# Two buffers for q and k, one PSUM buffer per product, and a reordered end in a sigmoid attention followed by a mixture of depths

## The chip, the cores and the metric

The kernel runs on one core of one Trainium2 chip. The metric is the device time of one execution in microseconds (us). Names of engines: PE is TensorE (PEld its weight loads), DVE is VectorE, ACT is ScalarE, POOL is GpSimd, SP is SyncE, which here only issues DMAs.

## The reference

```python
# q, k, v: (8, 12, 448, 64) float32;  capacity = 128;  D = 12*64 = 768;  F = 1024
scores = scale * np.matmul(q, k.transpose(0, 1, 3, 2)) - np.log(S)
attn = 1.0 / (1.0 + np.exp(-scores))
x = np.matmul(attn, v).transpose(0, 2, 1, 3).reshape(B, S, H * D)   # (8, 448, 768)

scores = np.einsum('bsd,d->bs', x, w_gate)
out = x.copy()
for b in range(B):
    top_idx = np.argpartition(-scores[b], capacity)[:capacity]      # 128 of 448 rows
    xe = x[b, top_idx]
    ye = np.maximum(xe @ w1, 0.0) @ w2                              # 768 -> 1024 -> 768
    g = 1.0 / (1.0 + np.exp(-scores[b, top_idx]))
    out[b, top_idx] = x[b, top_idx] + g[:, None] * ye
```

## The kernel before

**Attention.** The 96 heads are cut into 24 groups of four; a group is one index i of `load`, `turn` and `raws`. A stage s (0 to 11) works on groups 2s and 2s+1. `load(i)` fetches k and q of a group with two DMAs from SP, `turn(i)` transposes them on DVE into `kT` and `qT`, and a stage's seven `unit`s multiply q by k on PE into PSUM (line 269) and apply the sigmoid on ACT (line 277). `values` multiplies by v (line 304), one stage later for three of its four parts, into two PSUM tiles called `o`; `take` transposes the result on DVE into `x_b` (line 319), and that frees the `o` tiles.

**Choosing rows.** A batch b has three groups. When its x is whole, `gate` sums the scores, `spread` copies them over all partitions through DRAM (tile `rep`), `store` writes x to DRAM with four DMAs from SP, `ranking` counts on DVE how many scores are above each (lines 378 and 381), `place` sends the ranks through DRAM into `spot`, and `choose` finds the 128 rows and gathers them into `xe` with an indirect DMA from POOL. `copy_out` copies all of x to the output, and `scatter` overwrites the chosen rows at the end.

**The two products with w1 and w2.** Two batches (a pair p) are done together by a scheme of seven products of quarter matrices instead of eight: `first(p, key)` for w1, `second(p, key)` for w2, keys 1 to 7, each with sums before (rows in `rows_t`) and after (`first_sums`, `second_sums`, on DVE, ACT and POOL). The sums of weights are made once, kept in DRAM, and fetched by `lend` into attention tiles that are free for a while. `WORK` says at which stage and unit a product stands: (8, 5) is the gap behind unit 5 of stage 8, in which PE has nothing of the attention before the next unit. The last pairs follow in `rest`, after the attention.

**What sets the order.** The order of each engine is the order in the program; no scheduler moves anything, and semaphores make an engine wait where data or a buffer is missing. SP's DMAs stand in one line too: a DMA that waits holds up all behind it. DVE is likewise one line: `turn`, `ranking`, `take`, `gate_part` and the sums of products stand behind each other.

**Two places that the change touches.** In `raw` there is one buffer for k and one for q, so `load(i)` can start only when `turn(i-1)` has read the group before. And `bank` hands out the two halves of one PSUM tile to two products one after the other (`half`).

Of the kernel before, what the change touches and what calls it, by code (L numbers as in the profile page):

```python
# [9 lines left out]
F32 = mybir.dt.float32  # L10
# [7 lines left out]
def kernel(  # L18
# [40 lines left out]


    const = ctx.enter_context(tc.tile_pool(name="const", bufs=1))
    raw = ctx.enter_context(tc.tile_pool(name="raw", bufs=1))
    vals = ctx.enter_context(tc.tile_pool(name="vals", bufs=1))
    head = ctx.enter_context(tc.tile_pool(name="head", bufs=2))
    dram = ctx.enter_context(tc.tile_pool(name="dram", bufs=B, space=bass.MemoryType.DRAM))
# [24 lines left out]
    def load(i):  # L90

        if i >= NQ:
            return
        if i == 1:
            both = moe.tile([P, 7 * KH * P], F32, name="rows_t")
            raws[i] = [both[:, n * TB * Dh:(n + 1) * TB * Dh] for n in range(2)]
        else:
            raws[i] = [raw.tile([P, TB * Dh], F32, name=f"raw_{nm}") for nm in "kq"]
        for t, src in zip(raws[i], (k, q)):
            nc.sync.dma_start(  # L100
                out=t, in_=bass.AP(tensor=src.tensor, offset=src.offset + i * 4 * S * Dh,
                                   ap=[[TB * Dh, P], [1, TB * Dh]]))
# [40 lines left out]
    def load_weights(m):  # L143
        n = KH if m == 1 else FH
        w = (w1_sb, w2_sb)[m - 1]
        held = [(0, 0), (0, 1), (1, 1)] if m == 1 else [(0, 0), (1, 0), (1, 1)]
        left = (1, 0) if m == 1 else (0, 1)
        room = moe.tile([P, 7 * FH * P], F32, name="hidden")
        a, b = room[:, :QW], room[:, QW:2 * QW]
        c = moe.tile([P, 7 * KH * P], F32, name="rows_t")[:, :QW]  # L150
# [234 lines left out]
    def place(b):  # L385

        nc.vector.tensor_add(place_s[:, :NC], above, level)
        by_col = moe.tile([P, TT], F32, name="by_col")
        nc.vector.transpose(by_col, place_s)
        ranks = dram.tile([P, TT], F32, name="ranks")  # L390
        queue(b).dma_start(out=ranks, in_=by_col)
        spot = moe.tile([P, 4, NC * TT], F32, name="spot")
        queue(b).dma_start(
            out=spot, in_=bass.AP(tensor=ranks.tensor, offset=ranks.offset,
                                  ap=[[0, P], [TT * TT, 4], [1, NC * TT]]))
        st[b]["spot"] = spot.rearrange("p m c -> p (m c)")[:, :S]

    def choose(b):
# [19 lines left out]
            idx.append(at)  # L418
        gt = moe.tile([P, 1], F32, name="gate", bufs=4)
        nc.scalar.activation(gt[:n], picked[1][:n], AF.Sigmoid)  # L420
        xe = moe.tile([P, D], F32, name="xe", bufs=4)
        nc.gpsimd.indirect_dma_start(
            out=xe[:n], out_offset=None, in_=st[b]["x_d"][:, :],
            in_offset=bass.IndirectOffsetOnAxis(ap=row[:n, 0:1], axis=0))
        st[b].update(idx=idx, gate=gt, xe=xe)

    pairs, half = {}, [None]

    def bank(where):
        if half[0] is None:  # L430
            half[0] = banks(where)
            return half[0][:, 0]
        t, half[0] = half[0], None
        return t[:, 1]

    def turn_rows(b, where="o"):


        n = CAP
        p, odd = divmod(b, 2)  # L440
        if not odd:
            t = moe.tile([P, 7 * KH * P], F32, name="rows_t")
            pairs[p] = {"x": t.rearrange("p (m k n) -> p m k n", m=7, k=KH)}
# [12 lines left out]
        for dst, y, z in ((4, 2, 0), (2, 3, 2), (5, 3, 4), (6, 1, 5)):  # L456
            eng.tensor_tensor(out=x[:, dst, :, :n], in0=x[:, y, :, :n], in1=x[:, z, :, :n],
                              op=ALU.subtract)

    ROWS1 = {1: 0, 2: 1, 3: 3, 4: 6, 5: 4, 6: 5, 7: 2}

    def first(p, key, where="o"):
        n = CAP
# [85 lines left out]
    def scatter(b, m=None):  # L551
# [11 lines left out]

    WORK = {
# [10 lines left out]
    }  # L575

    LENT = {5: [(1, 7), (1, 6)], 6: [(1, 5), (1, 3), (2, 4)], 7: [(2, 5), (2, 6), (2, 7)],
            8: [(1, 7), (1, 6)], 9: [(1, 5), (1, 3)], 10: [(2, 4), (2, 5), (2, 6)],
            11: [(2, 7), (1, 7), (1, 6)]}

    def begin(item, where="o"):

# [5 lines left out]

    def do(item, where="o"):
        if item[0] == "t":  # L590
            half[0] = None
            turn_rows(item[1], where)
        elif item[0] == "s":
            for x in range(2):
# [40 lines left out]
    def gap(s, n):  # L635
        if n < 3 and s > 0:
            values(s - 1, n + 1)
            if n == 2:
                turns[0] = 1
                half[0] = None  # L640
# [59 lines left out]
    def stream():  # L700
        for b in range(B):
            routed(b)
        load(0)
        load(1)
        zero = moe.tile([P, NC * P], F32, name="spot")
        nc.vector.memset(zero, 0.0)
        nc.vector.memset(bias_s, NEG_LOG_S)
        turn(0)
        load(2)
        load_v(0)  # L710
        warm = banks(1)
        for _ in range(3):
# [51 lines left out]
```

## Time and profile before

| | |
|---|---|
| runs | 551.33, 552.72, 556.01 us; median 552.72 us |
| profiled execution | 556.21 us, of which the span of the trace is 554.2 us |
| mean granted PE clock of the span | 0.944 |
| busy: PE, PEld, DVE, ACT, POOL | 465.5, 273.7, 293.8, 184.6, 92.5 us |
| DMA | 104.19 MB, mean 188 GB/s |

A group of the profile names the line, the engine, the operation, out<-in tiles, the shape and the number of instructions. In a timeline a row is: start and length in us, engine, line, operation, tiles, and in brackets the idle time of that engine just ahead and what ended it. PE's full clock is 2.4 GHz, and 1.2 GHz is the lower of its two levels (granted clock 0.5).

### The profile page before, as it was taken

Reading aid. Unit: us, or ns where it says so; the run is one execution under the profiler, and the core shown is the slowest. Engines: PE = TensorE matmul, PEld = TensorE weight load, DVE = VectorE, ACT = ScalarE, POOL = GpSimd, SP = SyncE. Lnnn points to the kernel's source line nnn. Section 1 sums busy time; section 2 is a strip of 40 time slices with the busy share of each in tenths; the row PEclk is TensorE's granted clock in tenths of the full one; section 3 lists DMA queues with packets and bytes.
Section 4 is the critical chain, followed back from the end, with each engine's and each line's share of the span. In section 5 each row is a group of like instructions: output and inputs, shape, how many; then the busy total and the mean of one; then the engine's idle time right before and its main releaser. Section 6 shows DMA issues by size and latency. Waiting matters only on the chain. (4 is left out here: it accounts for less than half of the span.)

```text
span 554.2 us, 14369 instructions
## 1 busy us (share of the span) xinstructions
PE 465.5 (84%) x6326; PEld 273.7 (49%) x6326; DVE 293.8 (53%) x637; ACT 184.6 (33%) x240; POOL 92.5 (17%) x92
## 2 busy tenths in 40 slices
PE   8998839794998968985899997977998978586884
PEld 3554314362646534532446775543565467246842
DVE  3346593928529285428338385456445474542351
ACT  4754613452544531432253443341353201001000
POOL 7191560110000000400102000400001202411002
PEclk9999987896999988997999998998999997799998
DMA  8887996796277838674786837956567769816701
GB/s 258 282 270 266 334 246 180 132 263 144 49 243 189 168 82 245 109 240 148 170 294 180 146 118 190 165 215 195 134 209 189 144 175 237 308 34 234 278 14 43
DMA packets 134281, 104.19 MB, mean 188 GB/s; under 512 B 97996, under 2 KB 115644, under 8 KB 133964
## 3 DMA queue, kind: packets, MB, share of 16 engines
q1 hardware_dynamic: 130940, 89.07, 59.2%
q0 software_dynamic: 3280, 14.21, 8.4%
q8 instruction: 49, 0.80, 0.6%
q14 instruction: 12, 0.10, 0.1%
HBM read 82.67 MB, written 31.60 MB: 206 GB/s over the span
## 5 line engine op out<-in xcount | busy, mean ns | idle before, releaser
L269 PE MATMUL psc<-qT,kT 32*64 32x448 f32 x2496 | 161.0, 553 | 17.3 <-DVE qT L251 12.9
L304 PE MATMUL o<-attn_d,raw_v 32*64 32x448 f32 x1152 | 131.1, 541 | 0.6 <-ACT o L307 0.3
L304 PE MATMUL o<-attn_u,raw_v 32*64 32x448 f32 x1152 | 127.0, 540 | 1.4 <-ACT o L307 0.8
L277 ACT ACTIVATE attn_u<-psc,bias_s 128x896 f32<-128x896 f32 x86 | 81.9, 1004 | 121.4 <-PE psc L269 121.3
L269 PEld LDWEIGHTS psc<-qT,kT 32*64 32x64 f32 x2496 | 66.0, 134 | 82.8 <-issue 52.4
L277 ACT ACTIVATE attn_d<-psc,bias_s 128x896 f32<-128x896 f32 x70 | 66.7, 1004 | 57.8 <-PE psc L269 57.7
L304 PEld LDWEIGHTS o<-attn_u,raw_v 32*64 32x64 f32 x1152 | 51.3, 133 | 30.4 <-issue 21.0
L244 DVE STREAM_TRANSPOSE kT<-raw_k 128x384 f32<-128x384 f32 x46 | 23.8, 555 | 73.6 <-DMA raw_k<-in_k_dram 44.2
L304 PEld LDWEIGHTS o<-attn_d,raw_v 32*64 32x64 f32 x1152 | 50.2, 133 | 21.2 <-issue 18.9
L533 PE MATMUL o<-w_sb,hidden 128*128 128x384 f32 x72 | 34.9, 645 | 25.9 <-DVE x_b L319 15.6
L319 DVE STREAM_TRANSPOSE x_b<-o 128x448 f32<-128x448 f32 x48 | 26.8, 616 | 50.1 <-PE o L304 50.0
L544 DVE SCALAR_TENSOR_TENSOR xe<-o,gate,xe 128x384 f32<-128x384 f32 x43 | 24.5, 612 | 43.7 <-PE o L533 43.7
L474 PE MATMUL o<-rows_t,attn_d 128*128 128x128 f32 x264 | 36.0, 300 | 10.2 <-DVE hidden L484 5.7
L484 DVE TENSOR_TENSOR hidden<-o,hidden 128x512 f32<-128x512 f32 x25 | 16.7, 688 | 48.1 <-PE o L474 47.9
L474 PEld LDWEIGHTS o<-rows_t,attn_d 128*128 128x128 f32 x264 | 34.2, 213 | 15.0 <-DVE hidden L484 6.7
L533 PEld LDWEIGHTS o<-w_sb,hidden 128*128 128x128 f32 x72 | 17.3, 251 | 42.2 <-issue 34.1
L519 POOL TENSOR_TENSOR hidden<-hidden 128x512 f32<-128x512 f32 x12 | 16.5, 1393 | 129.8 <-ACT hidden L487 129.5
L327 DVE TENSOR_TENSOR scr<-x_b,wg_b 128x448 f32<-128x448 f32 x48 | 36.5, 761 | 1.0
L474 PE MATMUL o<-rows_t,w_sb 128*128 128x128 f32 x264 | 32.3, 279 | 3.4 <-ACT rows_t L451 1.9
L474 PEld LDWEIGHTS o<-rows_t,w_sb 128*128 128x128 f32 x264 | 30.3, 192 | 8.2 <-issue 3.1
L487 ACT ACTIVATE hidden<-hidden 128x512 f32<-128x512 f32 x15 | 9.5, 630 | 66.5 <-DVE hidden L484 66.5
L330 DVE TENSOR_REDUCE gate_p<-scr 128x14 f32<-128x448 f32 x48 | 29.8, 621 | 1.7
(102 smaller groups left out, 454.7 us busy)
## 6 DMA issues: line engine op xcount, KB each, us to landing
attn_d<-sum SPq DMA_DIRECT2D x52, 384.0 KB, 7.6
x_d<-x_b SPq DMA_DIRECT2D x32, 336.0 KB, 6.9
out_dram<-x_d SPq DMA_DIRECT2D x8, 1344.0 KB, 9.3
raw_k<-in_k_dram SPq DMA_DIRECT2D x23, 448.0 KB, 5.0
raw_q<-in_q_dram SPq DMA_DIRECT2D x23, 448.0 KB, 5.7
raw_v<-in_v_dram SPq DMA_DIRECT2D x48, 192.0 KB, 8.9
w_sb<-in_moe_w_dram SPq DMA_DIRECT2D x6, 768.0 KB, 12.4
sum<-hidden POOLq DMA_DIRECT2D x6, 768.0 KB, 6.4
```

What stands on the lines that cost most here:

```text
L244: nc.vector.transpose(kT[i][:, e, :HK], sk[:, e, :HK].rearrange("p (m c) d -> p c m d", c=NF))
L269: nc.tensor.matmul(psc[h // 2][y * Dh:(y + 1) * Dh, h % 2, :S], kT[2 * s + x][d, e, r:r + 2, :].rearrange("d r t -> d (r t)"), qT[2 * s + ...
L277: nc.scalar.activation(a, psc[pr][:, :, :S], AF.Sigmoid, bias=bias_s, scale=QK_SCALE)
L304: nc.tensor.matmul(o[x][j * Dh:(j + 1) * Dh, pr, :S], w, a[rows, j, :], start=(n == 0 and c == 0), stop=(n == 3 and c == NF - 1))
L319: nc.vector.transpose(x_tiles[b][:, :, 2 * g + pr, :], outs[s][x][:, pr, :S].rearrange("p (r t) -> p r t", t=TT))
L327: nc.vector.tensor_tensor(out=tmp, in0=x_tiles[b][:, :, hp, :], in1=wg_b[:, hp:hp + 1, :].to_broadcast([P, TB, TT]), op=ALU.mult)
L330: nc.vector.tensor_reduce(out=gate_parts[b][:, :, hp], in_=tmp, axis=AX.X, op=ALU.add)
L474: nc.tensor.matmul(ps[:, f, :n], w((t * FH + f) * P, P), x[:, t, :n], start=(t == 0), stop=(t == KH - 1))
L484: nc.vector.tensor_tensor(out=dst, in0=a, in1=b, op=ALU.add)
L519: nc.gpsimd.tensor_tensor(out=h[dst], in0=h[a], in1=h[b], op=op)
L533: nc.tensor.matmul(ps[:n, :DH], h[:, t, :n], w(t * DH, DH), start=(t == 0), stop=(t == FH - 1))
L544: nc.vector.scalar_tensor_tensor(out=xe[:n, cols], in0=ps[:n, :DH], scalar=st[b]["gate"][:n, 0:1], in1=xe[:n, cols], op0=ALU.mult, op1=ALU ...
```

## The change

Six things are edited.

1. `raw` has two buffers. `load` goes one group further ahead: three groups are asked for before the first `turn`, group 2 (not 1) uses the space of `rows_t` at the start, and behind `turn(2s+1)` stands `load(2s+3)`, behind `turn(2s+2)` stands `load(2s+4)`.
2. To make room, `rows_t` has six rows instead of seven (one sum of rows is made in place, over row 1, once the product that reads row 1 has been issued), and `xe` has three buffers instead of four, with the last batch's rows in a free attention tile.
3. Each product has a PSUM tile of its own (`bank`); the second half of it stays unused.
4. `WORK` and `LENT` put some products a step sooner; the last two products of the second pair's w2 now stand in stage 10.
5. In `rest`, all sums of `first` products stand ahead of `ranking`, the first product of w2 ahead of `choose`, and fewer weights are fetched ahead of `store`.
6. `ranks` and `spot` of the last batch go out from SP instead of POOL.

```diff
-    raw = ctx.enter_context(tc.tile_pool(name="raw", bufs=1))
+    raw = ctx.enter_context(tc.tile_pool(name="raw", bufs=2))
...
-        if i == 1:
-            both = moe.tile([P, 7 * KH * P], F32, name="rows_t")
+        if i == 2:
+            both = moe.tile([P, 6 * KH * P], F32, name="rows_t")
...
-        queue(b).dma_start(out=ranks, in_=by_col)
+        queue = nc.gpsimd if b < 2 else nc.sync
+        queue.dma_start(out=ranks, in_=by_col)
...
-        xe = moe.tile([P, D], F32, name="xe", bufs=4)
+        if b == B - 1:
+            xe = attn_tile(0, f"u{NU - 1}").rearrange("p a s -> p (a s)")[:, :D]
+        else:
+            xe = moe.tile([P, D], F32, name="xe", bufs=3)
...
     def bank(where):
-        if half[0] is None:
-            half[0] = banks(where)
-            return half[0][:, 0]
-        t, half[0] = half[0], None
-        return t[:, 1]
+        return banks(where)[:, 0]
...
-        for dst, y, z in ((4, 2, 0), (2, 3, 2), (5, 3, 4), (6, 1, 5)):
+        for dst, y, z in ((4, 2, 0), (2, 3, 2), (5, 3, 4)):
             eng.tensor_tensor(out=x[:, dst, :, :n], in0=x[:, y, :, :n], in1=x[:, z, :, :n],
                               op=ALU.subtract)
+        pairs[p]["turned"] = eng
+        last_row(p)
+    def last_row(p):
+        n = CAP
+        if pairs[p].get("turned") and pairs[p].get("second"):
+            x = pairs[p]["x"]
+            pairs[p]["turned"].tensor_tensor(out=x[:, 1, :, :n], in0=x[:, 1, :, :n],
+                                             in1=x[:, 5, :, :n], op=ALU.subtract)
...
-        (8, 3): [("t", 2), ("t", 3), (1, 1, 1)], (8, 4): [(1, 1, 2)],
-        (8, 5): [(1, 1, 7), (1, 1, 6)],
-        (9, 3): [(1, 1, 4)], (9, 4): [(1, 1, 5)], (9, 5): [(1, 1, 3), (2, 1, 1)],
+        (8, 3): [("t", 3), (1, 1, 1)], (8, 4): [(1, 1, 2), (1, 1, 7)],
+        (8, 5): [(1, 1, 6), (1, 1, 4)],
+        (9, 3): [(2, 1, 1), (2, 1, 2)], (9, 4): [(1, 1, 5)], (9, 5): [(1, 1, 3), (2, 1, 4)],
...
         ranking(b)
+        do((2, p, 1), "any")
         choose(b - 1)
-        for key in (1, 2, 3, 4, 5, 6):
+        for key in (2, 4, 5, 6):
             do((2, p, key), "any")
-        for key, slot in (((1, 5), "d02"), ((1, 3), "d10")):
-            lend(*key, slot)
         choose(b)
-        do((2, p, 7), "any")
+        for key in (7, 3):
+            do((2, p, key), "any")
...
         load(0)
         load(1)
+        load(2)
...
                     turn(2 * s + 1)
-                    if s > 0:
-                        load(2 * s + 2)
+                    load(2 * s + 3)
...
                     turn(2 * s + 2)
-                    load(2 * s + 3)
+                    load(2 * s + 4)
```

The first place is SP's line at the start of the program (`raw_k`, `raw_q` and, for one group, `rows_t` receive k and q; `raw_v` and `raw_h` receive v); one piece of the difference.

```order
+L100 DMA raw_k<-in_k_dram 128x896
+L100 DMA raw_q<-in_q_dram 128x896
 L100 DMA raw_k<-in_k_dram 128x896
 L100 DMA raw_q<-in_q_dram 128x896
 L100 DMA rows_t<-in_k_dram 128x896
 L100 DMA rows_t<-in_q_dram 128x896
+L119 DMA raw_v<-in_v_dram 32x8x192 x4
+L121 DMA raw_h<-in_v_dram 32x4x64 x4
 L100 DMA raw_k<-in_k_dram 128x896
 L100 DMA raw_q<-in_q_dram 128x896
-L119 DMA raw_v<-in_v_dram 32x8x192 x4
-L121 DMA raw_h<-in_v_dram 32x4x64 x4
```

One pair of DMAs more stands ahead of everything; from there on SP's pairs stand at the same places as before, but each fetches the group that comes one later.

The second place is PE in stage 6, gap 3, with the products (2, 0, 1) and (2, 0, 2); `o0` and `o1` are the two PSUM tiles, and a row's semaphores stand in brackets. Before:

```order
L269 MATMUL psc_2454<-qT_2328,kT_2327 64x448 x2
L533 MATMUL o0_2485<-w2_sb_88,hidden_1709 128x384 [waits DVE_49,PE_49]
L533 MATMUL o0_2485<-w2_sb_88,hidden_1709 128x384 x3
L533 MATMUL o0_2485<-w2_sb_88,hidden_1709 128x384 [waits DVE_49]
L533 MATMUL o0_2485<-w2_sb_88,hidden_1709 128x384 x3
```

Now:

```order
L269 MATMUL psc_2480<-qT_2354,kT_2353 64x448 x2
L546 MATMUL o0_2511<-w2_sb_88,hidden_1713 128x384 [waits DVE_49,PE_49]
L546 MATMUL o0_2511<-w2_sb_88,hidden_1713 128x384 x3
L546 MATMUL o1_2520<-w2_sb_88,hidden_1713 128x384 [waits DVE_49]
L546 MATMUL o1_2520<-w2_sb_88,hidden_1713 128x384 x3
```

The second product stands where it stood, but goes into the other tile, so what it waits for on DVE is the reader of that tile, not of its neighbour's sums.

The third place is DVE after the attention (`L378` to `L389` are the ranking of the last batch, `L405` or `L406` the choosing, `L484` or `L497` the sums of w1's products, `L544` or `L557` those of w2's). Before:

```order
L484 TENSOR_TENSOR hidden<-psc,hidden 128x512 x3
L484 TENSOR_TENSOR hidden<-o_4972,hidden 128x512 x3
L484 TENSOR_TENSOR hidden<-psc,hidden 128x512
L378 TENSOR_SCALAR scr,above<-rep,score 128x448
...
L389 STREAM_TRANSPOSE by_col<-place_s 128x32
L405 SCALAR_TENSOR_TENSOR scr,got<-spot,slot,number 128x448
L405 SCALAR_TENSOR_TENSOR scr,got<-spot,slot,rep 128x448
L410 CAST row<-got 128x1
L416 TENSOR_SCALAR idx<-got 128x1 x2
L544 SCALAR_TENSOR_TENSOR xe<-psc,gate,xe 128x384 x4
L544 SCALAR_TENSOR_TENSOR xe<-o_5072,gate,xe 128x384 x2
```

Now:

```order
L497 TENSOR_TENSOR hidden<-psc,hidden 128x512
L497 TENSOR_TENSOR hidden<-o_4998,hidden 128x512 x2
L378 TENSOR_SCALAR scr,above<-rep,score 128x448
...
L389 STREAM_TRANSPOSE by_col<-place_s 128x32
L557 SCALAR_TENSOR_TENSOR xe<-o_5072,gate,xe 128x384 x4
L406 SCALAR_TENSOR_TENSOR scr,got<-spot,slot,number 128x448
L406 SCALAR_TENSOR_TENSOR scr,got<-spot,slot,rep 128x448
L411 CAST row<-got 128x1
L417 TENSOR_SCALAR idx<-got 128x1 x2
L557 SCALAR_TENSOR_TENSOR xe<-psc,gate,xe 128x384
```

The first sums of w2's products have moved from behind the choosing to ahead of it; the ranking stays behind all sums of w1's.

## Rows read from the trace of the kernel before

**Rows 1.** Who waited for whom, whole span: us in total, times, longest.

```profile
PE psc L269 <- DVE qT L251: 12.9, 4, 9.2
DVE kT L244 <- DMA raw_k<-in_k_dram: 44.2, 9, 12.9
PE o L533 <- DVE xe L544: 13.4, 5, 6.3
```

**Rows 2.** Busy time by stretch (stage 6): length, busy us and instructions, clock, DMA share.

```profile
186.00:232.70 46.70, 39.08 (x528) 21.10 (x520) 26.58 (x61) 14.99 (x19) 5.02 (x4) 0.93 0.64 155
```

**Rows 3.** Timeline of SP, stages 3 and 4, and the end.

```profile
102.45 11.31 SPq L336 DMA_DIRECT2D x_d<-x_b  x4
117.13 0.53 SPq L100 DMA_DIRECT2D raw_k<-in_k_dram  x1
...
469.04 5.57 SPq L177 DMA_DIRECT2D attn_d<-sum  x6
```

**Rows 4.** Timeline of DVE, stage 4.

```profile
126.63 1.04 DVE L244 STREAM_TRANSPOSE kT<-raw_k 128x384 f32<-128x384 f32 x2 [12.93 <-DMA raw_k<-in_k_dram]
```

**Rows 5.** Timeline of PE, stages 3, 4, 6, 7, 9 and 10.

```profile
98.00 1.74 PE L269 MATMUL psc<-qT,kT 32*64 32x448 f32 x32
101.38 3.45 PE L269 MATMUL o<-qT,kT 32*64 32x448 f32 x26 [1.63 <-DVE x_b L319]
...
125.86 0.99 PE L269 MATMUL psc<-qT,kT 32*64 32x448 f32 x6
...
136.44 1.51 PE L448 MATMUL o<-iden,xe 128*128 128x128 f32 x6 [5.06 <-DVE x_b L319]
137.88 2.78 PE L269 MATMUL psc<-qT,kT 32*64 32x448 f32 x32
...
204.20 4.51 PE L533 MATMUL o<-w_sb,hidden 128*128 128x384 f32 x8 [4.43 <-DVE x_b L319]
210.99 4.54 PE L533 MATMUL o<-w_sb,hidden 128*128 128x384 f32 x8 [2.29 <-DVE xe L544]
...
255.02 5.03 PE L533 MATMUL o<-w_sb,hidden 128*128 128x384 f32 x8 [5.59 <-DVE x_b L319]
...
337.14 0.68 PE L474 MATMUL o<-rows_t,attn_d 128*128 128x128 f32 x4 [2.99 <-DMA attn_d<-sum]
...
367.69 2.89 PE L269 MATMUL psc<-qT,kT 32*64 32x448 f32 x30
376.16 4.20 PE L533 MATMUL o<-w_sb,hidden 128*128 128x384 f32 x8 [5.58 <-DVE x_b L319]
```

**Rows 6.** Timeline of DVE, stages 2 and 5.

```profile
70.00 6.92 DVE L353 COPY parts<-by_dim 32x32 f32<-32x32 f32 x4
...
177.36 2.00 DVE L484 TENSOR_TENSOR hidden<-o,hidden 128x512 f32<-128x512 f32 x3
```

**Rows 7.** Timeline of POOL, stage 2 and the end.

```profile
73.44 3.43 POOL L166 TENSOR_TENSOR hidden<-w_sb,rows_t 128x1536 f32<-128x1536 f32 x1
...
475.66 0.56 POOL L391 DMA_DIRECT2D ranks<-by_col  x1 [0.56 <-DVE by_col L389]
```

**Rows 8.** Timeline of PE, after the attention.

```profile
458.94 5.49 PE L474 MATMUL o<-rows_t,attn_d 128*128 128x128 f32 x24 [4.80 <-DVE hidden L484]
...
479.63 5.37 PE L533 MATMUL o<-w_sb,hidden 128*128 128x384 f32 x8 [6.32 <-DVE xe L544]
...
510.14 2.94 PE L474 MATMUL o<-rows_t,attn_u 128*128 128x128 f32 x24 [2.89 <-DVE rows_t L457]
```

**Rows 9.** DMA issues, whole span: tiles, queue, count, size, median us from issue to landing.

```profile
attn_d<-sum SPq DMA_DIRECT2D x52, 384.0 KB, 7.6
...
spot<-ranks SPq DMA_DIRECT2D x5, 256.0 KB, 6.5
...
xe<-x_d,row POOLq DMA_INDIRECT x8, 5.5
...
ranks<-by_col SPq DMA_DIRECT2D x5, 16.0 KB, 1.4
```

More of the change, by code (lines that the diff above doesn't have):

```diff
@@ L149, in load_weights @@
         a, b = room[:, :QW], room[:, QW:2 * QW]
-        c = moe.tile([P, 7 * KH * P], F32, name="rows_t")[:, :QW]
+        c = moe.tile([P, 6 * KH * P], F32, name="rows_t")[:, :QW]
         for dst, at in [(a, left)] + [(w[:, x], held[x]) for x in (2, 0, 1)]:
@@ L390, in place @@
         ranks = dram.tile([P, TT], F32, name="ranks")
-        queue(b).dma_start(out=ranks, in_=by_col)
+        queue = nc.gpsimd if b < 2 else nc.sync
+        queue.dma_start(out=ranks, in_=by_col)
         spot = moe.tile([P, 4, NC * TT], F32, name="spot")
-        queue(b).dma_start(
+        queue.dma_start(
             out=spot, in_=bass.AP(tensor=ranks.tensor, offset=ranks.offset,
@@ L425, in choose @@
         st[b].update(idx=idx, gate=gt, xe=xe)
-    pairs, half = {}, [None]
+    pairs = {}
     def bank(where):
-        if half[0] is None:
-            half[0] = banks(where)
-            return half[0][:, 0]
-        t, half[0] = half[0], None
-        return t[:, 1]
+        return banks(where)[:, 0]
     def turn_rows(b, where="o"):
@@ L441, in turn_rows @@
         if not odd:
-            t = moe.tile([P, 7 * KH * P], F32, name="rows_t")
-            pairs[p] = {"x": t.rearrange("p (m k n) -> p m k n", m=7, k=KH)}
+            t = moe.tile([P, 6 * KH * P], F32, name="rows_t")
+            pairs[p] = {"x": t.rearrange("p (m k n) -> p m k n", m=6, k=KH)}
         x = pairs[p]["x"]
@@ L455, in turn_rows @@
         eng = nc.vector if p in (0, NP - 1) else nc.gpsimd
-        for dst, y, z in ((4, 2, 0), (2, 3, 2), (5, 3, 4), (6, 1, 5)):
+        for dst, y, z in ((4, 2, 0), (2, 3, 2), (5, 3, 4)):
             eng.tensor_tensor(out=x[:, dst, :, :n], in0=x[:, y, :, :n], in1=x[:, z, :, :n],
                               op=ALU.subtract)
-    ROWS1 = {1: 0, 2: 1, 3: 3, 4: 6, 5: 4, 6: 5, 7: 2}
+        pairs[p]["turned"] = eng
[6 more added lines that the diff above has]
+                                             in1=x[:, 5, :, :n], op=ALU.subtract)
+    ROWS1 = {1: 0, 2: 1, 3: 3, 4: 1, 5: 4, 6: 5, 7: 2}
     def first(p, key, where="o"):
@@ L475, in first @@
                                  start=(t == 0), stop=(t == KH - 1))
+        if key == 2:
+            pairs[p]["second"] = True
+            last_row(p)
         return p, key, ps
@@ L565 @@
         (4, 3): [("t", 0)], (4, 4): [(1, 0, 1)], (4, 5): [(1, 0, 2)],
[9 rows of a table removed]
-    }
-    LENT = {5: [(1, 7), (1, 6)], 6: [(1, 5), (1, 3), (2, 4)], 7: [(2, 5), (2, 6), (2, 7)],
-            8: [(1, 7), (1, 6)], 9: [(1, 5), (1, 3)], 10: [(2, 4), (2, 5), (2, 6)],
-            11: [(2, 7), (1, 7), (1, 6)]}
[8 rows of a table added]
+    }
+    LENT = {5: [(1, 7), (1, 6), (1, 5)], 6: [(1, 3), (2, 4), (2, 5)], 7: [(2, 6), (2, 7)],
+            8: [(1, 7), (1, 6)], 9: [(1, 5), (1, 3), (2, 4)], 10: [(2, 5), (2, 6), (2, 7)],
+            11: [(1, 6), (1, 7), (1, 5)]}
     def begin(item, where="o"):
@@ L590, in do @@
         if item[0] == "t":
-            half[0] = None
             turn_rows(item[1], where)
@@ L639, in gap @@
                 turns[0] = 1
-                half[0] = None
                 for i, (m, key) in enumerate(LENT.get(s, ())):
@@ L661, in rest @@
             gap(NS, n)
-        room = [f"d1{i}" for i in range(3)] + [f"u{n}" for n in range(3, NU)] + ["d00"]
-        for key in ((1, 5), (1, 3)):
-            lend(*key, room.pop(0))
         p, b = NP - 2, B - 1
+        lend(1, 3, "d10")
         work = [(item, begin(item, "any")) for item in ((1, p, 6), (1, p, 7))]
@@ L670, in rest @@
         gate(waiting.pop())
-        for key in ((2, 4), (2, 5), (2, 6), (2, 7), (1, 7)):
-            lend(*key, room.pop(0))
+        for key, slot in (((2, 4), "d11"), ((2, 5), "d12"), ((2, 6), "u3"), ((2, 7), "u4")):
+            lend(*key, slot)
         for item, args in work:
@@ L677, in rest @@
             do((1, p, key), "any")
-        lend(1, 6, "d01")
+        for key, slot in (((1, 7), "u5"), ((1, 6), "d00"), ((1, 5), "d01"), ((1, 3), "d02")):
+            lend(*key, slot)
         ranking(b)
+        do((2, p, 1), "any")
         choose(b - 1)
-        for key in (1, 2, 3, 4, 5, 6):
+        for key in (2, 4, 5, 6):
             do((2, p, key), "any")
-        for key, slot in (((1, 5), "d02"), ((1, 3), "d10")):
-            lend(*key, slot)
         choose(b)
-        do((2, p, 7), "any")
+        for key in (7, 3):
+            do((2, p, key), "any")
         do(("s", p))
@@ L692, in rest @@
             do(item, "any")
-        for key, slot in (((2, 6), "d11"), ((2, 5), "d12"), ((2, 7), "u3"), ((2, 4), "u4")):
+        for key, slot in (((2, 6), "d10"), ((2, 5), "d11"), ((2, 7), "d12"), ((2, 4), "u3")):
             lend(*key, slot)
@@ L708, in stream @@
         turn(0)
-        load(2)
         load_v(0)
```

11 rows, old and new, of the table WORK are left out of this document.

## The prediction

> **What bounds the kernel.** I read the page's shares first: PE is busy 465.5 of 554.2 us, so the time is PE's work, its clock and its idle gaps. Then the list of waits [rows 1]. Its longest row is not PE's: DVE stands 44.2 us, nine times, for k. In SP's line the reason is plain: four stores of x take 11.31 us to issue, and the load of k comes out behind them, at 117.13 [rows 3]. It has only one buffer, so it could not have gone earlier either. DVE meets it at 126.63 after 12.93 us [rows 4]. Everything behind that `turn` on DVE is then late, `take` included, and PE stands for a free `o` tile: 5.06 us at 136.44, 4.43 at 204.20, 5.59 at 255.02, 5.58 at 376.16 [rows 5]. Each stop is followed by PE at half clock: 32 products at 137.88 take 2.78 us and those at 98.00 take 1.74; eight products of w2 take 4.51 to 5.03. At full clock I put those eight at 2.9: 24 products of w1 take 5.49 us at half clock and 2.94 at full, and 5.37 for eight of w2 goes down in that proportion [rows 8].
>
> The second kind of stop is the half-shared PSUM tile: a product waits for sums that read its neighbour's half. PE does so five times, 13.4 us [rows 1]: 2.29 at 210.99 [rows 5], 6.32 at 479.63 [rows 8], 4.8 in the other three (one in stage 7, two at the end).
>
> **Two buffers for q and k.** A load now comes one `turn` earlier, some 20 us, against 12.93 at most that it was late; so I let all stops behind it go. From the rows [5]:
> - Stage 3, at 101.38: 1.63 idle, 26 products at half clock in 3.45 instead of 26/32 of 1.74: 3.7, of which I take 3.3.
> - Stage 4: unit at 125.86 to the end of the next at 140.66 is 14.8; without waits 1.74 + 0.8 (six transposes, half of 1.51) + 1.74 = 4.3. Gain 10.5.
> - Stage 6: 4.43 + 2.29 idle (the second by the PSUM tile), 4.51 + 4.54 for 2 x 2.9: 10.0.
> - Stage 7: 5.59, and 5.03 for 2.9: 7.7; and 1.8 of the third PSUM wait.
> - Stage 9: 2.99 for a lent weight whose transfer stood behind the late ranking: 3.0.
> - Stage 10: 367.69 to 380.36 is 12.67 for 1.74 + 2.9: 8.0.
>
> Together 44.3 us.
>
> **What does not go.** The longest wait in the row of qT, 9.2 us [rows 1], looks like another late load and is not. Four copies of 32x32 on DVE take 6.92 us and end at 76.92; POOL's sum of weights, of 3.43 us, ends at 76.87 [rows 6, 7]. No part of the change touches either, so I leave it. The Trainium skill, "SBUF — State Buffer", "SBUF: two separate sides", says that VectorE and GpSimd share a port pair as an exclusive lock, and that the loser is blocked for the other's whole instruction. The two ends 0.05 us apart agree with it. Counted as a late load it would bring some 13 us more (the wait, and half clock after it).
>
> **New costs in the stages.** Product 4 of w1 now follows closely into the tile of product 7, whose sums stand on DVE: three sums take 2.00 us [rows 6]; I take 2.5 for both pairs. Products a step sooner leave less time to fetch their lent weights: 7.6 us from issue to landing [rows 9], and stage 6 already uses 0.64 of the DMA engines in 46.7 us [rows 2]; with a stage some 10 us shorter that is 0.82. Two or three places (stages 7, 9, 11) come to the edge: between 0 and 7.6 us each; I take 4 in all, nearer zero since only one such wait, of 2.99, shows among the rows of PE [rows 5], and that one behind a late ranking.
>
> **At no cost.** The row sum made in place waits for product 2 of w1; POOL or DVE makes it while PE does product 7, and without that cover it is one sum, under a us. Three buffers for `xe`: the gather of batch 3 waits for the scatter of batch 0, issued a good half stage before its transposes; uncovered it is one gather, 5.5 [rows 9]. The extra load at the start lies ahead of v, which nobody needs before stage 1; uncovered it is some us once.
>
> **The end.** Sums ahead of the ranking and tiles of their own remove 4.80 and 5.49 − 2.94 at 458.94, 6.32 and 5.37 − 2.9 at 479.63 [rows 8]. So the ranks, out at 475.66 [rows 7], would be ready 4.80 + 2.6 = 7.4 sooner, at 468.3. But they now go out from SP, where six lent weights are issued until 469.04 + 5.57 = 474.6 [rows 3]. From there: ranks land after 1.4 us in a free line or 7.6 behind lent weights, `spot` after 6.5, the gather after 5.5 [rows 9]. I take 7.6, since up to six such transfers stand ahead: 482.2, 488.7, 1.5 to choose (two operations over 448 columns at 0.67 each [rows 6], and small ones), gather landed at 495.7, transposes and row sums 0.8 + 2.89, first product of the last w1 on the new rows at 499.4. Before it was at 510.14 [rows 8]: 10.7 sooner. The two smaller PSUM waits behind it give 3 more; a PE that has stood is at half clock, 2 back. The end gives 12 us: 18 if the ranks land in 1.4, 5 if one more transfer of 7.6 stands ahead.
>
> The Trainium skill, "DMA: Bandwidth & Descriptors", "Queues, rings and completion order", says that each DMA engine serves the queues in turn, and one queue's descriptors in order. This speaks against moving the ranks from POOL's queue to SP's: on POOL's they would pass the lent weights. By it the end is at the 7.6, as taken; without it at the 1.4, 6 us sooner.
>
> **The sum.** 44.3 − 2.5 − 4 + 12 = 49.8, say 50. The profiled execution took 556.21, so 506.2; the median of the runs, 552.72, is 0.6% lower: 503.
>
> **Rivals.** *The DMA engines give half of it back.* Loads, lent weights and v come to the same queues in less time; at six places where weights are lent PE or DVE waits half of 7.6 us, 23 us: 526 (518 to 540). For it: the 0.82 above, and that a DMA held in SP's line holds up all behind it. Against: 188 GB/s and 104 MB stay what they were, and in stage 6 more than a third of the DMA time is free.
>
> *Slower: the tiles run short.* Two products shared a tile, and up to four could be open on two `o` tiles; now it is two. Every product then waits for the sums of the one two before it, and these stand on DVE behind `take`, `gate_part` and `ranking`. The price of one wait for DVE is there: 4.43 to 5.59 [rows 5], say 5. Some 14 products in the stages stand in a pair or right after one: 70 us, 573. From ten on it is slower than before. Against it: DVE is busy 26.58 of 46.70 us [rows 2], and its late line came from the loads, which go.
>
> *The change does not do what it says.* The load still stands behind `store` in SP's line, and if its `turn` comes when it always came, because something else (`rep`, the ranks) holds DVE at the same place, the waits only change their name. Then the gain is the end less the 6.5 of new costs: about 5 us, 547. Against: `turn(2s+3)` waited for k and for nothing else.
>
> **Chances.** Forecast (487 to 517) 0.74; half given back 0.13, of which 0.08 below 528; waits renamed 0.04; slower 0.03; below 487 0.06, by small half-clock stretches that I did not list. All gains at their ends, without new costs, are 44.3 + 18 = 62, 491; with 4 us for the unlisted ones 487. Range 487 to 528. A measurement of this kernel tells about 1% (its runs span 551.3 to 556.0): faster 0.93, same 0.03, slower 0.04.
>
> **What would show it.** Right: DVE's row for raw_k falls from 44.2 to under 10; PE's waits for `x_b` in stages 3 to 10 are gone, and the stages from 3 to 10 are each 3 to 10 us shorter, at a granted clock nearer 1; the wait of 9.2 is still there; PE waits some us for `hidden` in stage 8, gap 5; at the end the longest wait of PE is for the last batch's gather, with the ranks landed some 14 us after DVE made them. Half given back: waits of PE for lent weights or v, or of DVE for `rep`, at several places. Tiles short: PE waiting for `hidden` or `xe` at most products in the stages. The forecast is wrong if the row of raw_k stays above 20, or if it goes and the stages keep their length.

## The result, and the profile after

| | before | after |
|---|---|---|
| median of 4 runs, us | 552.79 (551.33 to 556.01) | 510.53 (509.28 to 511.81) |
| profiled execution, us; span | 556.21; 554.2 | 509.84; 507.7 |
| granted PE clock | 0.944 | 0.956 |
| busy PE, us; PE idle (span less busy) | 465.5; 88.7 | 450.2; 57.5 |

The ratio is 0.9228 (0.918 to 0.9276): faster by 42 us, where 50 were forecast. All ratios below leave slow executions out; the profiled execution was such a one in two experiments (the first pair's order of before, 522.63 us, and spot behind the lent weights, 503.07 us), so their rows are read for what waits for what, not for lengths. The list of waits after the change (who waits for whom: us in total, times, longest) answers to [rows 1]:

```profile
PE o L546 <- DMA attn_d<-sum: 14.0, 3, 6.6
PE psc L269 <- DVE qT L251: 10.5, 2, 9.6
PE o L484 <- ACT rows_t L451: 9.1, 1, 9.1
...
DVE kT L244 <- DMA raw_k<-in_k_dram: 3.2, 2, 2.7
```

DVE's 44.2 us for k are 3.2, and `x_b` and `xe` are gone from PE's rows. The 9.6 in stage 2 stays. New at the top are lent weights, and one stop of 9.1 behind ACT. On PE's timeline:

```profile
239.52 5.45 PE L546 MATMUL o<-attn_d,hidden 128*128 128x384 f32 x8 [6.61 <-DMA attn_d<-sum]
...
246.59 2.85 PE L546 MATMUL o<-attn_d,hidden 128*128 128x384 f32 x8
...
286.48 2.92 PE L484 MATMUL o<-rows_t,w_sb 128*128 128x128 f32 x24 [2.20 <-DVE hidden L497]
...
352.01 8.10 PE L546 MATMUL o<-attn_d,hidden 128*128 128x384 f32 x16 [4.48 <-DMA attn_d<-sum]
...
431.30 4.23 PE L546 MATMUL o<-attn_d,hidden 128*128 128x384 f32 x8 [2.96 <-DMA attn_d<-sum]
...
455.92 4.81 PE L484 MATMUL o<-rows_t,w_sb 128*128 128x128 f32 x24 [9.14 <-ACT rows_t L451]
...
466.96 3.31 PE L484 MATMUL psc<-rows_t,attn_u 128*128 128x128 f32 x14 [2.89 <-DVE rows_t L457]
```

Eight products take 2.85 us at a granted clock of 1.00, and 5.45 right behind a stop, where it is 0.51; so a stop of 6.61 costs 9.2.

The length of a stage is taken from its first sigmoid (ACT, line 277) to that of the next; stage 11 runs to the first product after the attention (445.83 and 409.14). Work that changed its stage is counted at 2.8 us a product and 0.85 for six transposes.

| stage | before | after | work moved | difference without it | forecast |
|---|---|---|---|---|---|
| 3 | 29.2 | 24.9 | 0 | -4.3 | -3.3 |
| 4 | 38.7 | 29.4 | 0 | -9.3 | -10.5 |
| 5 | 33.4 | 38.9 | +2.8 | +2.7 | 0 |
| 6 | 46.7 | 35.3 | 0 | -11.4 | -10.0 |
| 7 | 46.1 | 39.9 | -2.0 | -4.2 | -9.5, less lent weights |
| 8 | 36.9 | 39.3 | +2.0 | +0.4 | +2.5 |
| 9 | 39.9 | 35.4 | +2.8 | -7.4 | -3.0 |
| 10 | 44.0 | 39.8 | 0 | -4.2 | -8.0, less lent weights |
| 11 | 44.3 | 38.3 | -5.6 | -0.5 | 0 |

To the end of the attention that is 36.7 us (37.8 forecast; stages 0 to 2 are 1.4 longer), and 9.8 after it (12 forecast).

### The profile page after: what moved, and what is told of

Read it like the earlier page. It is cut to its first block, busy times and chain, and to the rows that moved or that the text cites. A ratio compares the mean times of both kernels' runs of the same rounds, so it can differ in the third digit from the quotient of the medians.

```text
span 507.7 us, 14392 instructions
## 1 busy us (share of the span) xinstructions
PE 450.2 (89%) x6326; PEld 261.2 (51%) x6326; DVE 292.6 (58%) x637; ACT 184.4 (36%) x240; POOL 90.9 (18%) x90
## 5 line engine op out<-in xcount | busy, mean ns | idle before, releaser
L269 PE MATMUL psc<-qT,kT 32*64 32x448 f32 x2496 | 150.0, 546 | 15.4 <-DVE qT L251 10.5
L304 PE MATMUL o<-attn_d,raw_v 32*64 32x448 f32 x1152 | 128.8, 536 | 1.4 <-issue 1.0
L304 PE MATMUL o<-attn_u,raw_v 32*64 32x448 f32 x1152 | 123.5, 535 | 0.8 <-ACT o L307 0.8
L269 PEld LDWEIGHTS psc<-qT,kT 32*64 32x64 f32 x2496 | 58.9, 132 | 80.8 <-issue 55.3
L546 PE MATMUL o<-attn_d,hidden 128*128 128x384 f32 x88 | 37.1, 578 | 14.0 <-DMA attn_d<-sum 14.0
L557 DVE SCALAR_TENSOR_TENSOR xe<-o,gate,xe 128x384 f32<-128x384 f32 x40 | 22.6, 610 | 34.9 <-PE o L546 34.9
L484 PE MATMUL o<-rows_t,w_sb 128*128 128x128 f32 x216 | 28.2, 291 | 12.6 <-ACT rows_t L451 9.1
L327 DVE TENSOR_TENSOR scr<-x_b,wg_b 128x448 f32<-128x448 f32 x48 | 38.3, 798 | 1.0
L484 PE MATMUL o<-rows_t,attn_d 128*128 128x128 f32 x288 | 34.5, 277 | 1.2 <-DVE rows_t L457 1.2
L484 PEld LDWEIGHTS o<-rows_t,attn_d 128*128 128x128 f32 x288 | 33.0, 192 | 4.8 <-DVE rows_t L457 2.0
L484 PEld LDWEIGHTS o<-rows_t,w_sb 128*128 128x128 f32 x216 | 26.7, 204 | 16.8 <-ACT rows_t L451 9.4
L546 PEld LDWEIGHTS o<-attn_d,hidden 128*128 128x128 f32 x88 | 19.0, 223 | 30.9 <-issue 22.4
L497 DVE TENSOR_TENSOR hidden<-o,hidden 128x512 f32<-128x512 f32 x24 | 15.9, 687 | 31.5 <-PE o L484 31.3
L378 DVE TENSOR_SCALAR_CACHE_REDUCE scr<-rep,score 128x448 f32<-128x448 f32 (+1 forms) x32 | 21.5, 672 | 11.4 <-DMA rep<-scores 10.6
```

What stands on the lines that cost most here:

```text
L269: nc.tensor.matmul(psc[h // 2][y * Dh:(y + 1) * Dh, h % 2, :S], kT[2 * s + x][d, e, r:r + 2, :].rearrange("d r t -> d (r t)"), qT[2 * s + ...
L304: nc.tensor.matmul(o[x][j * Dh:(j + 1) * Dh, pr, :S], w, a[rows, j, :], start=(n == 0 and c == 0), stop=(n == 3 and c == NF - 1))
L327: nc.vector.tensor_tensor(out=tmp, in0=x_tiles[b][:, :, hp, :], in1=wg_b[:, hp:hp + 1, :].to_broadcast([P, TB, TT]), op=ALU.mult)
L378: nc.vector.tensor_scalar(out=junk[:n], in0=rep[:n], scalar1=own, scalar2=0.0, op0=ALU.is_gt, op1=ALU.add, accum_out=above[:n, c:c + 1])
L497: nc.vector.tensor_tensor(out=dst, in0=a, in1=b, op=ALU.add)
L546: nc.tensor.matmul(ps[:n, :DH], h[:, t, :n], w(t * DH, DH), start=(t == 0), stop=(t == FH - 1))
```

## Experiments: undoing one edit

Each kernel is the changed one with one edit taken back. Differences are those of the ratios to the kernel before, times 553 us.

**One buffer for q and k** (`raw` with one buffer, the loads where they were).

```diff
-    raw = ctx.enter_context(tc.tile_pool(name="raw", bufs=2))
+    raw = ctx.enter_context(tc.tile_pool(name="raw", bufs=1))
...
-                    load(2 * s + 3)
+                    if s > 0:
+                        load(2 * s + 2)
...
-                    load(2 * s + 4)
+                    load(2 * s + 3)
```

> The changed kernel with one buffer for k and q and the loads where they were before; all other edits stay. Theory (the loads' second buffer brings nearly all of the gain in the stages): the waits of DVE for k come back, above 35 us in the list, the stops of PE for x_b with them, and of the 37 us that the attention became shorter some 30 go again: 538 to 548 us. Rival (the order of products and the PSUM tiles brought it, and the late loads were a symptom): under 522 us, with the row of raw_k long and PE not waiting for x_b.

Measured: 537.38 us, ratio 0.9714 (0.9669 to 0.9759), 27 us slower than the changed kernel. Its list of waits:

```profile
PE psc L269 <- DVE qT L251: 22.6, 5, 7.9
PE o L546 <- DVE x_b L319: 9.5, 3, 4.2
...
PE o L448 <- DVE x_b L319: 5.8, 1, 5.8
...
PE o L546 <- DMA attn_d<-sum: 3.0, 2, 2.5
...
DVE kT L244 <- DMA raw_k<-in_k_dram: 68.0, 11, 18.0
```

The waits for k come back, longer than before (68.0 for 44.2; what makes them longer is open), and the stops of PE with them. In this order of products the second buffer carries 27 of the 42 us; the forecast gave it about 40. In the 27 the new waits for lent weights are already taken off: with one buffer PE stands 3.9 us for them (the row of 3.0 and another of 0.9), with two 14.0. Expected were 538 or more; the rival's 522 is far off.

**Shared PSUM tiles.**

```diff
     def bank(where):
-        return banks(where)[:, 0]
+        if half[0] is None:
+            half[0] = banks(where)
+            return half[0][:, 0]
+        t, half[0] = half[0], None
+        return t[:, 1]
```

> The changed kernel with the two halves of a PSUM tile given to two products again; all other edits stay. Theory (a product waits for the sums that read its neighbour's half): PE waits for xe and hidden return, in the end and in the gaps with two products, 10 to 16 us in all with half clock behind some: 520 to 527 us. Rival (tiles of one's own leave only two products open, so that sharing would be as good or better): 505 to 512 us.

Measured: 523.75 us, ratio 0.9452 (0.9392 to 0.9513), 12 us slower. PE's timeline of it, one place in stage 9 and one behind the attention:

```profile
311.88 2.85 PE L550 MATMUL o<-w_sb,hidden 128*128 128x384 f32 x8 [2.73 <-DVE xe L561]
...
424.49 5.49 PE L488 MATMUL o<-rows_t,attn_d 128*128 128x128 f32 x24 [4.89 <-DVE hidden L501]
```

The stop of 4.89 is the 4.80 of [rows 8], with 24 products at half clock behind it again. A tile of its own for each product pays, and the rival of too few tiles is out: in the changed kernel PE waits for a product's sums twice, 3.1 us in all.

**The first pair's order of before.**

```diff
-        (5, 3): [("t", 1)], (5, 4): [(1, 0, 7), (1, 0, 6)], (5, 5): [(1, 0, 4), (1, 0, 5)],
-        (6, 3): [(2, 0, 1), (2, 0, 2)], (6, 4): [(1, 0, 3)], (6, 5): [(2, 0, 4), (2, 0, 5)],
+        (5, 3): [("t", 1)], (5, 4): [(1, 0, 7), (1, 0, 6)], (5, 5): [(1, 0, 4)],
+        (6, 3): [(2, 0, 1), (2, 0, 2)], (6, 4): [(1, 0, 5)], (6, 5): [(1, 0, 3), (2, 0, 4)],
...
```

> The changed kernel with the first pair's products and lent weights in stages 5 to 8 at their places of before; the second and third pair's stay. Theory (with the loads on time the places of products only move PE work between stages, and the wait for a lent weight in stage 7 comes from SP's line, where the fetch of spot stands for the ranks ahead of all lent weights): the same sum of products, a wait for a lent weight of 4 to 8 us in stage 7 again, 508 to 514 us. Rival (a step sooner is what costs the wait): the wait in stage 7 is gone and the time is 502 to 506 us. Second rival (a step sooner is itself a gain): 515 us or more.

Measured: 514.82 us (509.85 to 522.63), ratio 0.9264 (0.9211 to 0.9318), which overlaps that of the changed kernel: no difference that can be told, so what the new places of the first pair bring or cost is at most some 6 us. The wait for a lent weight in stage 7 is there in its rows (8.88 us at 247.57), so a product a step sooner is not what makes it, and the first rival is out. The places of the second and third pair weren't tried alone.

**The last batch's ranks from POOL.**

```diff
-        queue = nc.gpsimd if b < 2 else nc.sync
+        queue = nc.gpsimd if b < 2 or b == B - 1 else nc.sync
```

> The changed kernel with the last batch's ranks and spot on POOL's queue as before. Theory (in SP's line the ranks stood 6.9 us behind lent weights, 433.3 to 440.2, and took 8.5 more to land): the ranks go out at about 433.5 and land within 5 us, spot is there about 445 instead of 453.5, so the end is some 6 us shorter, less 2 to 3 because the gather of batch 6 stands behind spot in POOL's line: 505 to 508 us. Rival (POOL's line is the later one, which is why the move pays): 512 to 518 us.

Measured: 506.45 us, ratio 0.9134 (0.9083 to 0.9185), some 5 us faster, by intervals that just touch; the rows go the same way. First SP in the changed kernel, then POOL in this one:

```profile
433.43 6.10 SPq L177 DMA_DIRECT2D attn_d<-sum  x6
440.20 0.32 SPq L392 DMA_DIRECT2D ranks<-by_col  x1
448.71 0.37 SPq L394 DMA_DIRECT2D spot<-ranks  x1
```

```profile
435.45 0.55 POOL L392 DMA_DIRECT2D ranks<-by_col  x1 [4.11 <-DVE by_col L389]
441.21 0.76 POOL L394 DMA_DIRECT2D spot<-ranks  x1 [5.20 <-DVE xe L557]
442.27 1.02 POOL L426 DMA_INDIRECT xe<-x_d,row  x1 [0.30 <-issue]
450.38 0.99 POOL L426 DMA_INDIRECT attn_u<-x_d,row  x1 [7.08 <-PE psc L448]
```

From SP the ranks go out 4.75 us later and `spot` 8.5 behind them; from POOL it is 5.8. The gather of batch 6 stands behind `spot` in POOL's line, 442.27 for 437.06, which takes a part back; PE's first product on the new rows comes at 463.12 for 466.96. So edit 6 made the kernel slower, as far as these tell. By the Trainium skill, "DMA: Bandwidth & Descriptors", "Queues, rings and completion order", a DMA engine serves its queues in turn and one queue's descriptors in order; the run went that way in the 5.8 for 8.5, while the 4.75 is SP's own line.

The four edits taken back one by one come to 27 + 12 + 0 - 5, or 34 of the 42 us. The reordered end (edit 5) wasn't taken back alone, so what it brings, and what the edits bring only together, stays open.

## Experiments: the stops that are left

**Spot behind the lent weights.** SP's line of the changed kernel in stage 7:

```profile
218.90 0.53 SPq L100 DMA_DIRECT2D raw_k<-in_k_dram  x1
...
221.53 0.46 SPq L100 DMA_DIRECT2D raw_q<-in_q_dram  x1
223.15 0.33 SPq L392 DMA_DIRECT2D ranks<-by_col  x1
231.63 0.38 SPq L394 DMA_DIRECT2D spot<-ranks  x1
232.14 3.59 SPq L177 DMA_DIRECT2D attn_d<-sum  x4
```

SP stands 8.5 us for the ranks to land (6.4 in stage 10), and the lent weights come out behind. In the kernel before it stood 1.4 in both stages:

```profile
246.68 0.33 SPq L100 DMA_DIRECT2D raw_k<-in_k_dram  x1
247.67 0.33 SPq L100 DMA_DIRECT2D raw_q<-in_q_dram  x1
253.75 0.33 SPq L391 DMA_DIRECT2D ranks<-by_col  x1
255.18 0.38 SPq L393 DMA_DIRECT2D spot<-ranks  x1
```

There the second pair of loads was held by its one buffer until 246.68, and the last load left 6 us ahead of the ranks; now four loads leave in the 4 us just ahead of them (in stage 10 in the 6 us). With one buffer again (first experiment) `spot` goes out 1.5 and 1.4 us behind the ranks in these stages. So the second buffer itself made the ranks late. The edit, `fetch` being the second DMA of `place`:

```diff
         put(s + 1, 1, ranking, b)
+        put(s + 1, 2, fetch, b)
```

> The changed kernel with the fetch of spot issued one gap later, behind the lent weights in SP's line (in the end it follows the ranks as before). Theory (in stages 7 and 10 SP stands 8.5 and 6.4 us for the ranks to land before it may issue spot, and the lent weights behind it come late): the waits of PE of 6.61 and 4.48 us go or fall below 2, and the half clock behind them: 497 to 502 us. Rival (the lent weights are late because their attention tiles come free late, or because the DMA engines are full): both waits stay above 4, 508 to 513 us.

Measured: 496.6 us, ratio 0.8944 (0.8904 to 0.8985), 15.7 us faster by the ratio. SP's line of it:

```profile
229.35 0.52 SPq L392 DMA_DIRECT2D ranks<-by_col  x1
231.72 2.64 SPq L177 DMA_DIRECT2D attn_d<-sum  x4
238.40 0.37 SPq L398 DMA_DIRECT2D spot<-ranks  x1
```

Of 14.0 us for lent weights 3.5 are left, 3.1 of them at the end; in the first and third combination below it is 4.2 and 3.7. The rival (attention tiles free late, or DMA engines full) is out: a change of place in SP's line is enough.

**The gate's sigmoid later.** ACT in the changed kernel:

```profile
454.97 0.20 ACT L421 ACTIVATE gate<-got 128x1 f32<-128x1 f32 x1 [18.01 <-DVE scr L406]
455.08 0.79 ACT L451 ACTIVATE rows_t<-psc 128x768 f32<-128x768 f32 x1
```

The copy of batch 6's transposes, done on PE at 446.8, stands behind a sigmoid of batch 7 that waits for `spot`.

```diff
-        nc.scalar.activation(gt[:n], picked[1][:n], AF.Sigmoid)
+        def weigh():
+            nc.scalar.activation(gt[:n], picked[1][:n], AF.Sigmoid)
...
         for item in (("t", b - 1), (1, p, 1), (1, p, 2), ("t", b)):
             do(item, "any")
+        st[b]["weigh"]()
```

> The changed kernel with the sigmoid of the last batch's gate moved behind the transposes of its rows on ACT. Theory (the wait of 9.14 us at the end is ACT's line: the copy of batch 6's transposes stands behind a sigmoid that waits for spot, so PE has nothing though the rows of batch 6 are there): the first two products of the last w1 run from about 447, the wait moves to the gather of batch 7, landed at 459.6, and the new rows' first product comes at 463.5 instead of 467: 506 to 509 us, with a wait of 5 to 7 us for attn_u. Rival (PE waits for the gather of batch 7 itself, as forecast): no change, 509 to 512 us, the wait of 9 us at the same place.

Measured: 507.05 us, ratio 0.9149 (0.9117 to 0.9182), 4.4 us faster, by intervals that just touch. PE's timeline of it:

```profile
447.86 2.94 PE L491 MATMUL o<-rows_t,w_sb 128*128 128x128 f32 x24 [0.96 <-ACT rows_t L458]
...
459.90 1.51 PE L455 MATMUL o<-iden,attn_u 128*128 128x128 f32 x6 [6.41 <-DMA attn_u<-x_d,row]
463.64 4.88 PE L491 MATMUL psc<-rows_t,attn_u 128*128 128x128 f32 x24 [2.23 <-DVE rows_t L464]
```

The two products run at once and the gather becomes the wait, as expected.

**The copies of the first gate on ACT.**

```diff
-            nc.vector.tensor_copy(parts[:, a], by_dim[a * TT:(a + 1) * TT])
+            if b:
+                nc.vector.tensor_copy(parts[:, a], by_dim[a * TT:(a + 1) * TT])
+            else:
+                nc.scalar.activation(parts[:, a], by_dim[a * TT:(a + 1) * TT], AF.Copy)
```

> The changed kernel with the four copies of 32x32 of the first batch's gate on ACT instead of DVE. Theory (on DVE they are held by POOL's sums of weights, so the turn behind them is late): the copies take under 1 us each, the wait of 9.56 us of PE in stage 2 falls below 3, and half clock goes with it: 498 to 503 us. Rival (the turn is late for another reason, its load or the transposes themselves held in the same way): a wait above 6 stays, 507 to 512 us.

Measured: 511.03 us, ratio 0.9218 (0.9151 to 0.9285): no difference. ACT, DVE and PE of it:

```profile
70.99 0.94 ACT L356 ACTIVATE parts<-by_dim 32x32 f32<-32x32 f32 x4 [6.15 <-DVE by_dim L350]
```

```profile
74.08 4.26 DVE L327 TENSOR_TENSOR scr<-x_b,wg_b 128x448 f32<-128x448 f32 x1
```

```profile
74.82 1.94 PE L269 MATMUL psc<-qT,kT 32*64 32x448 f32 x10 [7.73 <-ACT attn_u L277]
```

The copies take 0.94 us, but ACT waits for DVE with the units behind it, and the next multiplication, 0.62 elsewhere, takes 4.26 beside POOL. PE's stop of 9.56 is one of 7.73 under another name. Not the copies alone are held.

**POOL's sums in quarters.**

```diff
-            nc.gpsimd.tensor_tensor(out=dst, in0=x, in1=y, op=op)
+            for part in range(4):
+                cut = slice(part * QW // 4, (part + 1) * QW // 4)
+                nc.gpsimd.tensor_tensor(out=dst[:, cut], in0=x[:, cut], in1=y[:, cut], op=op)
```

> The changed kernel with each of POOL's eight sums of weights cut into four of a quarter of the columns. Theory (an operation of DVE that meets one of POOL's stands until that one ends, whatever it is: copies and multiplications alike): a piece takes about 0.9 us, so each DVE operation is held by at most that, the copies of 6.9 us take 2 to 4, the wait of 9.56 us in stage 2 falls to 2 to 5: 500 to 507 us. Rival (DVE and POOL share by bandwidth, so the same columns cost DVE the same time in pieces): the wait stays above 7, 508 to 513 us.

Measured: 513.13 us, ratio 0.9259 (0.9194 to 0.9324): no gain. DVE and POOL of it:

```profile
66.34 1.06 DVE L329 TENSOR_TENSOR scr<-x_b,wg_b 128x448 f32<-128x448 f32 x1
...
70.03 7.75 DVE L355 COPY parts<-by_dim 32x32 f32<-32x32 f32 x4
...
78.44 4.57 DVE L365 COPY score<-by_token 32x4 f32<-32x4 f32 x4
```

```profile
64.01 4.25 POOL L168 TENSOR_TENSOR hidden<-hidden,w_sb 128x384 f32<-128x384 f32 x4 [17.52 <-DMA w_sb<-in_moe_w_dram]
...
69.15 3.86 POOL L168 TENSOR_TENSOR rows_t<-w_sb,hidden 128x384 f32<-128x384 f32 x4
...
73.89 3.85 POOL L168 TENSOR_TENSOR hidden<-hidden,w_sb 128x384 f32<-128x384 f32 x4
```

A multiplication beside the pieces of the first sum now takes 1.06 (3.65 beside a whole sum in the changed kernel), the copies are held as before: they end at 77.78, the last piece of POOL's third sum at 77.74. PE's stop in stage 2 is 10.57, above 7 as the rival had it.

**The turn ahead of the gate**, in stage 2 behind unit 3.

```diff
+                if (s, n) == (2, 3):
+                    turn(2 * s + 2)
                 gap(s, n)
                 if n == NU - 2:
-                    turn(2 * s + 2)
+                    if s != 2:
+                        turn(2 * s + 2)
```

> The changed kernel with the first transposes for stage 3 put ahead of the first batch's gate on DVE, in stage 2 behind unit 3; POOL's sums and DVE's copies stay as they are. Theory (the stop of 9.56 us is only DVE's line: copies held by POOL stand ahead of a turn that itself is held by nothing, since its k and q have been there since long): the copies still take about 7 us, the turn is done by 67, the stop in stage 2 goes: 498 to 503 us. Rival (the transposes are held by POOL too, or stage 3 then stops at its ranking): a stop above 6 in stage 2 or 3, 507 to 512 us.

Measured: 511.42 us, ratio 0.9224 (0.9161 to 0.9288): no difference, as the rival had it. PE, DVE and POOL of it:

```profile
100.22 3.50 PE L269 MATMUL o<-qT,kT 32*64 32x448 f32 x26 [12.29 <-DVE x_b L319]
```

```profile
92.54 0.68 DVE L378 TENSOR_SCALAR_CACHE_REDUCE scr<-rep,score 128x448 f32<-128x448 f32 x1 [8.40 <-DMA rep<-scores]
```

```profile
78.86 0.54 POOL L358 DMA_DIRECT2D scores<-total  x1
86.59 0.58 POOL L370 DMA_DIRECT2D rep<-scores  x1 [7.20 <-DMA scores<-total]
```

The stop in stage 2 is gone, and one of 12.29 stands in stage 3: `take` is behind the ranking of batch 0, whose scores leave behind POOL's sums at 78.86 and are back as `rep` at 92.5. Two things meet there, and taking away the first shows the second. A ranking put behind `take` in stage 3 would be the next trial; it wasn't made.

**Combinations.** The first has spot behind the lent weights, the late sigmoid, the copies on ACT, and this at the end:

```diff
-        for key, slot in (((1, 7), "u5"), ((1, 6), "d00"), ((1, 5), "d01"), ((1, 3), "d02")):
-            lend(*key, slot)
         ranking(b)
+        fetch(b)
+        for key, slot in (((1, 7), "u5"), ((1, 6), "d00"), ((1, 5), "d01"), ((1, 3), "d02")):
+            lend(*key, slot)
```

> The three edits (spot behind the lent weights, the late gate sigmoid, the copies on ACT) together, and the last batch's ranks and spot issued ahead of the four lent weights that only the last pair needs. Theory (the four stops are separate): 11 for the lent weights, 10 for the copies, 9 at the end, together 30 less some overlap: 478 to 486 us. Rival (a stop that goes is replaced by the next line, the DMA engines or DVE): 490 us or more.

Measured: 488.18 us, ratio 0.8792 (0.8741 to 0.8843). The second has the quarters in place of the copies on ACT, and four lent weights ahead of the stores of x at the end:

```diff
+        for key, slot in (((2, 4), "d11"), ((2, 5), "d12"), ((2, 6), "u3"), ((2, 7), "u4")):
+            lend(*key, slot)
         store(b)
         gate(waiting.pop())
-        for key, slot in (((2, 4), "d11"), ((2, 5), "d12"), ((2, 6), "u3"), ((2, 7), "u4")):
-            lend(*key, slot)
```

> Spot behind the lent weights, the late gate sigmoid, the last batch's ranks ahead of the last pair's lent weights, POOL's sums in quarters, the copies back on DVE, and in the end the first four lent weights ahead of the four stores of x. Theory (each stop by itself): 488 us of the combination before, less 5 to 8 in stage 2 by the pieces and 2 to 4 for the lent weight at the end: 477 to 482 us. Rival (the stores behind lent weights make the gathers late, or the pieces bring nothing): 486 to 492 us.

Measured: 493.45 us, ratio 0.8878 (0.8828 to 0.8928), no better than the first. The third is the first with the early turn in place of the copies on ACT:

> The early turn, spot behind the lent weights, the late gate sigmoid, and the last batch's ranks and spot ahead of the last pair's lent weights, together. Theory (four separate stops): 511 less 14 for spot, 10 for the turn and 10 at the end: 476 to 481 us. Rival (with the copies still at 7 us the score of the first batch is late, and its ranking holds up stages 3 and 4): 484 to 490 us.

Measured: 488.03 us, ratio 0.8812 (0.8767 to 0.8857). PE's waits, one line of each in this order:

```profile
PE psc L269 <- ACT attn_u L277: 13.7, 6, 10.2
```

```profile
PE psc L271 <- DVE qT L253: 15.6, 2, 12.0
```

```profile
PE o L269 <- DVE x_b L319: 8.9, 1, 8.9
```

All three theories promised too much (478 to 486, 477 to 482, 476 to 481); only the third's rival has the time in its range. Spot had brought 15.7 us alone, and the first combination brings 8.4 more, at the end, where PE's longest stop is 3.3 us for 9.1. The stop in stage 2 stays in every form: 10.2 us behind ACT in the first, 12.0 in the second, and 8.9 in stage 3 in the third. First and third beat the changed kernel by 24 and 23 us.

## Why the prediction was nearly right, by its steps

- **Where the line starts.** Right in sign and mechanism: the second buffer frees DVE's line, and its going back returns 27 us, of 36 forecast (40 less the 4 for lent weights).
- **New cost by lent weights: 4 us.** This is the term that was mis-sized: PE's stops in stages 7 and 10 measured 11.1 us and the half clock behind them 5.0 (5.45 for 2.85, 8.10 for 5.70), some 16 together. I priced it as a transfer of 7.6 us on its edge and found zero nearer, since before the change only one wait of 2.99 showed. What came late was `spot`, which waits in SP's line for the ranks to land, ahead of all lent weights. The median of 1.4 us for the ranks [rows 9] was right for the kernel before. The change made it 8.5, by the four loads that now leave just ahead of the ranks; I counted what two buffers free, not what their loads then stand in front of.
- **Stops and half clock.** Stage 9 gave 7.4 without moved work, 3.0 forecast: I counted the stop of 2.99, and not two short ones of 0.30 and 0.78 nor the half clock behind it. Stages 7 and 10 gave 8.4 of 17.5, where 4 in all were put aside for lent weights. Small gains in stages 3, 6, 8 and 9 made up for that, so the attention came out at 36.7 for 37.8; that is luck, two errors cancelled.
- **Product 4 behind product 7.** 2.5 forecast for both pairs; 2.20 measured at stage 8, gap 5, and 0.86 for the first pair at stage 5, 3.1 together. Stage 5 is 2.7 longer without moved work, of which the rest is not explained.
- **The wait of 9.2 that stays.** Right, 9.6 after. That POOL holds DVE there is borne out by the copies (0.94 on ACT) and the multiplication. The Trainium skill, "SBUF — State Buffer", "SBUF: two separate sides", has such a lock, held for one whole instruction; with POOL's sums in quarters a copy stood through four of them, 3.0 to 4.3 us, which is more than that. What I claimed it would bring if removed, 13 us, is wrong: the early turn removed it and brought nothing.
- **The end.** 12 forecast, 9.8 measured. Counted from the end of the attention the gather landed at 50.5 us, 49.9 forecast, though its parts were off (the ranks 8.5 for 7.6, `spot` 4.8 for 6.5, the gather 3.9 for 5.5). But the new rows' first product stood at 57.8, 53.6 forecast: I let the two products of batch 6 run ahead of the gather, and they waited in ACT's line. Moving the ranks to SP cost some 5. The queue rule had the direction; of the 7.5 us that `spot` leaves later, 4.75 are SP's line, which the sum held, and 2.7 the landing.
- **Scale.** 510.5 for 503: 3.6 us are the sum (46.4 for 50 between the profiled executions). The rest is the step to the median: the profiled execution before lay 3.4 above its median, for which I took 3.2 off, and that after lay 0.7 below.

## What to carry to other kernels

When a late load is mended, look in the same issue line for the next transfer that waits for another's landing, and put what PE needs ahead of it: here one DMA issued a gap later was worth some 15 us. A load that may leave earlier also stands ahead of something new: here four loads came to stand just ahead of 16 KB of ranks, whose landing went from 1.4 to 8.5 us. A long stop with one name can have a second cause of the same length behind it; move the first before pricing its removal. A small operation that waits for data (a sigmoid of 128 numbers) holds a whole engine's line.

## What was not expected of the hardware

POOL's sums in four pieces hold DVE's 32x32 copies as whole sums would. The four copies take 0.72 us together elsewhere; in that run two of them stood through a sum each, 3.02 and 4.34 us, and ended 0.05 and 0.04 us after its last piece, though one piece takes 1.0. The other two passed in 0.17 each between the sums. The pieces leave no gap, each starting some 0.05 us before the one ahead of it ends. Yet a multiplication beside such pieces took 1.06, and 0.63 and 0.66 in the second combination (3.65 beside a whole sum). Why the one gets in between and the other not is open.
